# Attention's exponentials left unscaled until the output, its longest key block reduced over two banks, and the MLP run in four width groups

## The chip, the cores and the metric

The kernel runs on one core of a Trainium2 chip. A core has TensorE (PE in the profile, with its weight loads in a row of their own, PEld), VectorE (DVE), ScalarE (ACT), GpSimd (POOL) and SyncE (SP), which here issues the DMAs. Each engine takes its own instructions in the order in which they stand. SBUF is the working memory; PSUM, into which TensorE writes, has eight banks of 512 fp32 columns. The metric is the device time of one execution in microseconds (us).

## The reference

Three stages follow each other, all in fp32: block-causal attention, an MLP with a leaky ReLU, and a mixture of eight experts whose gates are normalised in eight rounds.

```
attention: B=4, H=8, S=576, D=64
scores = (q @ k.T) / sqrt(D), masked so that query block i sees key blocks 0..i (blocks of 64)
attn = exp(scores - max)
attn = attn / (sum(attn) + 1e-09)
x = attn @ v                         # 2304 tokens x 512
MLP: x = max(0.01 * h, h) @ w_out    # h = x @ w_in, 512 -> 2048 -> 512
experts: P = gates(x @ w_gate); out = sum over e of P[:, e] * (relu(x @ w1[e]) @ w2[e])
```

The MLP's weights come as words of another format (pairs of 32-bit words) and are turned into fp32 on the chip, eight elementwise steps for each unit of 128 columns.

## The kernel before, in words

**Attention** goes over 16 pairs of heads (four batches, four pairs each). In a pair, query block i has its scores for 64(i+1) keys made in one matmul (`score`, L313; two heads stand beside each other in the 128 output rows). Block 8, with 576 keys, doesn't fit one bank and is made as two matmuls of 288 columns in two tiles, with two maxima, two exponentials, one minimum (L317) and one sum (L324). VectorE takes the maximum of a score tile (L314), ScalarE the exponential with its running sum (L319). `normalise` then turns the sums of three blocks at a time into reciprocals (L329 on GpSimd, L330 on VectorE) and multiplies the exponentials by them in place: blocks 8 to 5 on VectorE (L337), block 4 on ScalarE (L335), blocks 3 to 0 on GpSimd (L337). The scaled exponentials are transposed on TensorE in seven groups of up to four 128x128 squares (`turn_attn`, L344), copied out of PSUM (five groups on ScalarE, L351, two on VectorE, L353) and multiplied with v (`weigh`, L366 and L369), which gives the pair's 128 features by 576 queries in a tile `av` of two banks. `split_x` writes this as a rounded high part (ScalarE, L382) and the rest (VectorE, L383). All matmuls up to here are in fp32; in the MLP and behind it each operand is a high and a low part in fp32r, and three products take the place of one.

PSUM in this stage: three banks for scores (`ps_sc`), three for transposes (`ps_tr`), two for `av`. The scores of pair p+1, the transposes and products of pair p and the q and k of pair p+2 are written side by side in one loop (`turns` lists what stands beside each score); the scheduler that builds the program then sets the order of instructions on each engine. The steps that turn the MLP's weights into fp32 (`bits_steps`) are dealt out over this loop, ten units in all.

**MLP** in two groups of 1024 hidden columns (eight units f of 128). In a group the five token blocks (three of 512 tokens, two of 384) follow each other; for each f `hidden` makes 12 matmuls (L510) and four elementwise instructions, `second` 12 matmuls (L539) into four banks that gather the eight f. At the end of a block the four banks are drained into `xa`: copied in group 0 (L548, L550), added in group 1 (L552). The weights of group 1 are turned to fp32 beside group 0, stored to DRAM (`s_in`, `s_out`), loaded again and split. The pools of this stage are opened after those of attention are closed. The last block runs beside the steps that open the experts (`x_step`, `gate_chunk`, `w1_sums`).

**Experts** (L735 and L789) take the rest of the time, and the change touches only which pool their weights come from.

Of the kernel before, what the change touches and what calls it, by code (L numbers as in the profile page):

```python
# [15 lines left out]
P = 128  # L16
BLK = 64
# [19 lines left out]
def block_attention_mlp_moe(  # L37
# [24 lines left out]
    FC = 8  # L62
    NG = DFF // (FC * P)
# [16 lines left out]
    w1pool = ctx.enter_context(tc.tile_pool(name="w1pool", bufs=4))  # L80
    wpools = {1: [w1pool, w1pool]}
    dram = ctx.enter_context(tc.tile_pool(name="dram", bufs=1, space=bass.MemoryType.DRAM))
# [18 lines left out]

    s_in = dram.tile([DM, (NG - 1) * FC * P], F32, name="s_in")
    s_out = dram.tile([(NG - 1) * FC * P, DM], F32, name="s_out")
    w_raw, w_part = {}, {}

    def w_load(which, e, j, pool=None):
        raw = (pool or rawpool).tile([P, 1024], F32, name="wraw", tag="wraw")
        f0 = 2 * j * P
        if which == 1:
            src = s_in[:, (e - 1) * FC * P + f0:(e - 1) * FC * P + f0 + 2 * P] if e < NG else w1[e - NG][:, f0:f0 + 2 * P]  # L110
            nc.sync.dma_start(
                out=raw.rearrange("p (c f) -> p c f", c=KC), in_=src.rearrange("(c p) f -> p c f", p=P)
            )
        else:
            src = s_out[(e - 1) * FC * P + f0:(e - 1) * FC * P + f0 + 2 * P, :] if e < NG else w2[e - NG][f0:f0 + 2 * P, :]
            nc.sync.dma_start(
                out=raw.rearrange("p (j d) -> p j d", j=2), in_=src.rearrange("(j p) d -> p j d", p=P)
            )
        w_raw[which, e, j] = raw

    def w_tiles(which, e, j):
        pool = wpools[which][min(j, 1)]
# [23 lines left out]
    def bits_steps(which, f):  # L146
# [35 lines left out]
        def rest():  # L182
            bf = st["bf"] = (st["b"] if f < FC else st["low"]).bitcast(F32)
# [22 lines left out]
        def store():  # L206
            a = st["af"]
            nc.gpsimd.tensor_tensor(out=a, in0=a, in1=st["bf"], op=ALU.add)
            g = slice((f - FC) * P, (f - FC + 1) * P)
            if which == 1:  # L210
                nc.sync.dma_start(out=s_in[:, g].rearrange("(c p) f -> p c f", p=P), in_=chunks(a))
            else:
                nc.sync.dma_start(out=s_out[g, :], in_=a)

        return [begin, bound, shift, sign, power, rest] + ([parts, low_part] if f < FC else [store])


    def attention(att, ps_sc, ps_tr, ps_av):
# [10 lines left out]
        nmax = [att.tile([P, NQ + 1], F32, name=f"nmax{i}") for i in range(2)]  # L229
        ssum = [att.tile([P, NQ + 1], F32, name=f"ssum{i}") for i in range(2)]  # L230
        rsum = [att.tile([P, NQ + 1], F32, name=f"rsum{i}") for i in range(2)]
# [68 lines left out]
        turn_order = [8, 0, 7, 1, 6, 2, 5, 3, 4]  # L300
        col = {i: n + 1 for n, i in enumerate(turn_order)}

        latest = [None]

        def score(p, i):
            n = BLK * (i + 1)
            cuts = [(0, n)] if n <= 512 else [(0, n // 2), (n // 2, n)]
            part = []
            nm, sm = nmax[p % 2], ssum[p % 2]
            x = col[i]  # L310
            for s, (lo, hi) in enumerate(cuts):
                sc = ps_sc.tile([P, 512], F32, name="sc", tag="sc")[:, 0:hi - lo]
                nc.tensor.matmul(sc, qbd[p % 2][:, i, :], kT[p % 2][:, lo:hi], start=True, stop=True)  # L313
                latest[0] = nc.vector.tensor_reduce(out=nm[:, x - s:x - s + 1], in_=sc, axis=AX.X, op=ALU.max, negate=True)  # L314
                part.append(sc)
            if len(cuts) > 1:
                nc.vector.tensor_tensor(out=nm[:, x:x + 1], in0=nm[:, x:x + 1], in1=nm[:, x - 1:x], op=ALU.min)  # L317
            for s, (lo, hi) in enumerate(cuts):
                nc.scalar.activation(  # L319
                    out=ex[p % 2][:, off[i] + lo:off[i] + hi], in_=part[s], func=AF.Exp,  # L320
                    bias=nm[:, x:x + 1], scale=1.0, accum_out=sm[:, x - s:x - s + 1],
                )
            if len(cuts) > 1:
                nc.gpsimd.tensor_tensor(out=sm[:, x:x + 1], in0=sm[:, x:x + 1], in1=sm[:, x - 1:x], op=ALU.add)  # L324

        def normalise(p, lo, hi):
            r, s, e = rsum[p % 2], ssum[p % 2], ex[p % 2]
            c = slice(lo + 1, hi + 1)
            nc.gpsimd.tensor_scalar(out=r[:, c], in0=s[:, c], scalar1=EPS, scalar2=None, op0=ALU.add)  # L329
            nc.vector.reciprocal(out=r[:, c], in_=r[:, c])  # L330
            for i in turn_order[lo:hi]:
                a = e[:, off[i]:off[i] + BLK * (i + 1)]
                x = r[:, col[i]:col[i] + 1]
                if i == 4:
                    nc.scalar.activation(out=a, in_=a, func=AF.Copy, scale=x)  # L335
                else:
                    (nc.gpsimd if i < 4 else nc.vector).tensor_scalar(out=a, in0=a, scalar1=x, scalar2=None, op0=ALU.mult)  # L337

        def turn_attn(p, g):
# [10 lines left out]
            if n == 4 and g not in (5,):  # L350
# [22 lines left out]

        def split_x(p):
            b, hp = divmod(p, NPAIR)
            x = av.pop(p)[:, o:o + S]
# [619 lines left out]
```

## Time and profile before

| | |
|---|---|
| time, median of 3 runs (lowest, highest) | 2136.92 us (2135.82, 2139.2) |
| time of the profiled execution | 2137.32 us |
| its span, first to last instruction | 2135.5 us |
| TensorE matmul rows busy | 2114.1 us, 99% of the span |
| TensorE weight loads busy | 1842.6 us, 86% |
| VectorE, ScalarE, GpSimd busy | 1434.7, 915.0, 500.9 us |
| mean granted TensorE clock | 0.999 |

Busy time is the time that an engine's instructions cover. Matmuls overlap one another and their ends are modelled, so that a full row of TensorE says only that it never stood without a matmul; what one costs is read from the distance between the starts of neighbours. Attention ends 234 us into the span, the MLP between 605 and 650 us, where it overlaps the start of the experts.

### The profile page before, as it was taken

The numbers are of one execution on the slowest core, as the hardware profiler recorded it, in microseconds if no ns is written. First come the engines' busy times: TensorE is split into PE (matmuls) and PEld (weight loads), VectorE is DVE, ScalarE is ACT, GpSimd is POOL, SyncE is SP. The second block draws the span as 40 slices with busy tenths as digits, with TensorE's granted clock in tenths as the row PEclk, the third lists the DMA queues.
The fourth block names the chain that finished last, engine by engine and source line by source line (L and its number), as shares of the span: only waits on it lengthen the run. The fifth ranks groups of instructions, "written<-read, shape, count | busy, mean of one in ns | idle before, by whom it ended". The sixth has DMA issues, their size and how long they took to land.

```text
span 2135.5 us, 29009 instructions
## 1 busy us (share of the span) xinstructions
PE 2114.1 (99%) x10772; PEld 1842.6 (86%) x10772; DVE 1434.7 (67%) x2347; ACT 915.0 (43%) x1900; POOL 500.9 (23%) x587
## 2 busy tenths in 40 slices
PE   8999999999999999999999999999999999999999
PEld 5665688988899889989998998899899989988998
DVE  7887656644367876667678666766678676667665
ACT  7886422232234344344444434443444344344432
POOL 3444311200031222122123212222222222122120
PEclk9999999999999999999999999999999999999999
DMA  4442122420011221222123122212222221222120
GB/s 113 97 99 74 56 70 75 120 63 1 1 47 53 79 78 41 79 79 64 56 89 99 50 69 79 77 43 79 80 61 88 79 79 48 71 79 73 47 79 30
DMA packets 157245, 146.59 MB, mean 69 GB/s; under 512 B 62640, under 2 KB 126128, under 8 KB 157104
## 3 DMA queue, kind: packets, MB, share of 16 engines
q1 hardware_dynamic: 157104, 144.75, 22.8%
q8 instruction: 84, 1.38, 0.3%
q14 instruction: 57, 0.47, 0.1%
HBM read 135.81 MB, written 8.91 MB: 68 GB/s over the span
## 4 chain that ended last, share of the span: by engine, by line
PE 95%; DVE 3%; ACT 1%; issue 0%; DMA 0%; POOL 0%; SPq 0%; ACTq 0%; POOLq 0%; DVEq 0%
PE o L789 36%; PE h_ps L735 33%; PE o L539 9%; PE h_ps L510 9%; PE sc L313 3%; PE av L369 2%; PE tr L344 2%; DVE ex L337 0%; DVE w1l L693 0%; DVE nmax L314 0%; PE km L286 0%; ACT ex L319 0%; PE qm L280 0%; PE av L366 0%; DMA wraw<-in_moe_w_out_dram 0%
## 5 line engine op out<-in xcount | busy, mean ns | idle before, releaser
L789 PE MATMUL o<-w2h,xhlate 128*128 128x512 f32 x1152 | 402.6, 390 | 0.0
L789 PE MATMUL o<-w2h,xllate 128*128 128x512 f32 x1152 | 401.6, 389 | 0.0
L676 POOL TENSOR_TENSOR wa<-wraw 128x256 f32<-128x256 f32 x96 | 88.7, 924 | 1252.4 <-DVE w1l L693 1214.7
L743 ACT COPY s<-h_ps 128x384 f32<-128x384 f32 x288 | 138.1, 480 | 538.7 <-PE h_ps L735 538.5
L752 DVE TENSOR_TENSOR c<-h_ps,s 128x384 f32<-128x384 f32 x288 | 155.6, 554 | 311.0 <-PE h_ps L735 301.0
L735 PE MATMUL h_ps<-xhS,w1h 128*128 128x384 f32 x768 | 257.1, 335 | 0.0
L735 PE MATMUL h_ps<-xlS,w1h 128*128 128x384 f32 x768 | 256.5, 334 | 0.0
L735 PE MATMUL h_ps<-xhS,w1l 128*128 128x384 f32 x768 | 256.5, 334 | 0.0
L789 PEld LDWEIGHTS o<-w2h,xllate 128*128 128x128 f32 x1152 | 216.3, 188 | 45.4
L789 PEld LDWEIGHTS o<-w2h,xhlate 128*128 128x128 f32 x1152 | 216.3, 188 | 43.4
L789 PE MATMUL o<-w2l,xhlate 128*128 128x512 f32 x576 | 224.7, 390 | 0.0
L789 PE MATMUL o<-w2l,xllate 128*128 128x512 f32 x576 | 224.4, 390 | 0.0
L802 DVE SCALAR_TENSOR_TENSOR xa<-o,pr,xa 128x512 f32<-128x512 f32 x264 | 189.1, 740 | 50.4 <-PE o L789 50.4
L735 PE MATMUL h_ps<-xhA,w1l 128*128 128x384 f32 x576 | 193.0, 335 | 0.0
L735 PE MATMUL h_ps<-xhA,w1h 128*128 128x384 f32 x576 | 193.0, 335 | 0.0
L735 PE MATMUL h_ps<-xlA,w1h 128*128 128x384 f32 x576 | 192.7, 335 | 0.0
L693 DVE TENSOR_TENSOR w1l<-wraw,w1h 128x512 fp32r<-128x512 f32 x192 | 172.9, 938 | 0.1
L693 DVE TENSOR_TENSOR w1l<-wa,w1h 128x512 fp32r<-128x512 f32 x192 | 161.9, 845 | 0.0
L758 ACT ACTIVATE xllate<-c 128x384 fp32r<-128x384 f32 x144 | 75.7, 526 | 183.4 <-DVE c L752 183.4
L132 DVE TENSOR_TENSOR w2l<-wraw,w2h 128x1024 fp32r<-128x1024 f32 x100 | 145.6, 1456 | 6.7 <-ACT w2h L131 6.7
L735 PEld LDWEIGHTS h_ps<-xhS,w1h 128*128 128x128 f32 x768 | 144.2, 188 | 0.1
L735 PEld LDWEIGHTS h_ps<-xlS,w1h 128*128 128x128 f32 x768 | 144.2, 188 | 0.0
(158 smaller groups left out, 4064.9 us busy)
## 6 DMA issues: line engine op xcount, KB each, us to landing
wraw<-in_moe_w_dram SPq DMA_DIRECT2D x192, 512.0 KB, 4.3
wraw<-in_moe_w_in_dram SPq DMA_DIRECT2D x16, 512.0 KB, 3.8
wraw<-in_moe_w_out_dram SPq DMA_DIRECT2D x16, 512.0 KB, 3.8
out_dram<-xa SPq DMA_DIRECT2D x18, 256.0 KB, 2.0
qraw<-in_q_dram SPq DMA_DIRECT2D x32, 128.0 KB, 2.8
kraw<-in_k_dram SPq DMA_DIRECT2D x32, 128.0 KB, 2.4
vraw<-in_v_dram SPq DMA_DIRECT2D x32, 128.0 KB, 2.4
s_in<-wa SPq DMA_DIRECT2D x8, 256.0 KB, 2.4
```

The lines of the kernel that those rows point to most:

```text
L132: nc.vector.tensor_tensor(out=lo, in0=raw, in1=f32(hi), op=ALU.subtract)
L313: nc.tensor.matmul(sc, qbd[p % 2][:, i, :], kT[p % 2][:, lo:hi], start=True, stop=True)
L510: nc.tensor.matmul(ps[:, 0:n], w[:, c, cols], x, start=c == 0 and s == 0, stop=c == KC - 1 and s == 2,)
L539: nc.tensor.matmul(o_ps[s][:, 0:n], w[:, cut], h[:, 0:n], start=f == 0 and m == 0, stop=f == FC - 1 and m == 2)
L676: nc.gpsimd.tensor_tensor(out=one[:, 0], in0=a21, in1=a22, op=ALU.add)
L693: nc.vector.tensor_tensor(out=lo, in0=x, in1=f32(hi), op=ALU.subtract)
L735: mm = nc.tensor.matmul(ps, w[:, c], x[:, c], start=first and c == 0 and s == 0, stop=c == 1 and s == 2, skip_group_check=True,)
L743: nc.scalar.copy(out=t, in_=bank[n, name][:, 0:HT])
L752: nc.vector.tensor_tensor(out=c, in0=x, in1=part[n, add], op=ALU.add)
L758: nc.scalar.activation(out=hi, in_=x, func=AF.Relu),
L789: mm = nc.tensor.matmul(o, h, w, start=m == 0, stop=m == 11)
L802: nc.vector.scalar_tensor_tensor(out=a, in0=o, scalar=pr[:, tt, e:e + 1], in1=a, op0=ALU.mult, op1=ALU.add)
```

## The change

In attention the exponentials are transposed and multiplied with v as they are. The reciprocals of a pair's nine totals are made at once (`totals`). GpSimd multiplies them into a 128x576 tile `by_query`, whose row r holds the reciprocals of the queries q with q = r modulo 64 and zeros elsewhere (`place_totals`). Two fp32 matmuls with a 128x128 matrix of ones for each head (`both_heads`) then give the reciprocals of all 576 queries on each head's 64 feature rows: 512 columns into a bank of `ps_tr`, 64 into a free corner of the `av` tile (`spread_totals`). They are copied to SBUF (`by_feature`), and `split_x` first multiplies `av` by them into `xs`, from which the high part (ScalarE) and the rest (now on GpSimd) are made.

The score tiles become pairs of banks, two pairs in all: block 8 fills one pair and has one maximum and one exponential over both banks; blocks 7 and 0, 6 and 1, 5 and 2, 4 and 3 share a pair. `ps_tr` has two banks in place of three. ScalarE copies transposed groups 0 and 3, VectorE the other five.

The MLP goes in four groups of 512 hidden columns; groups 2 and 3 leave out the last token block, which then runs once over all eight units of both. The weights of groups 1 to 3 are turned into fp32 parts straight into their tiles, five steps at a time beside the runs before them, without the way over DRAM. In attention eight units are turned in place of ten. `bits_steps` loses its last alternative (`store`). The later pools are opened with `reuse_waits="tile"`, by which a tile waits for those that it overlaps, not for the whole pool before it.

```diff
         def score(p, i):
             n = BLK * (i + 1)
-            cuts = [(0, n)] if n <= 512 else [(0, n // 2), (n // 2, n)]
...
-                sc = ps_sc.tile([P, 512], F32, name="sc", tag="sc")[:, 0:hi - lo]
...
+            place = next(some.index(i) for some in shares if i in some)
+            if place == 0:
+                bank[p] = ps_sc.tile([P, 2, 512], F32, name="sc", tag="sc")
...
+            latest[0] = nc.vector.tensor_reduce(out=nm, in_=sc, axis=axes, op=ALU.max, negate=True)
+            nc.scalar.activation(out=to, in_=sc, func=AF.Exp, bias=nm, scale=1.0, accum_out=sm)
...
-        def normalise(p, lo, hi):
-            r, s, e = rsum[p % 2], ssum[p % 2], ex[p % 2]
...
-                if i == 4:
-                    nc.scalar.activation(out=a, in_=a, func=AF.Copy, scale=x)
-                else:
-                    (nc.gpsimd if i < 4 else nc.vector).tensor_scalar(out=a, in0=a, scalar1=x, scalar2=None, op0=ALU.mult)
+        def totals(p):
+            r, s = rsum[p % 2], ssum[p % 2]
+            nc.gpsimd.tensor_scalar(out=r, in0=s, scalar1=EPS, scalar2=None, op0=ALU.add)
+            nc.vector.reciprocal(out=r, in_=r)
+
+        def place_totals(p):
+            nc.gpsimd.tensor_tensor(
+                out=by_query.rearrange("p (i q) -> p i q", q=BLK),
+                in0=one_head.unsqueeze(1).to_broadcast([P, NQ, BLK]),
+                in1=rsum[p % 2].unsqueeze(2).to_broadcast([P, NQ, BLK]), op=ALU.mult,
+            )
...
-            if n == 4 and g not in (5,):
+            if g in (0, 3):
                 nc.scalar.copy(out=dst, in_=tr[:, 0:n])
             else:
                 nc.vector.tensor_copy(out=dst, in_=tr[:, 0:n])
...
+        def spread_totals(p):
+            t, rb = av[p], ps_tr.tile([P, 512], F32, name="rb", tag="tr")
+            nc.tensor.matmul(rb, both_heads, by_query[:, 0:512], start=True, stop=True)
+            nc.tensor.matmul(t[:, 0:S - 512], both_heads, by_query[:, 512:S], start=True, stop=True)
+            nc.scalar.copy(out=by_feature[:, 0:512], in_=rb)
+            nc.vector.tensor_copy(out=by_feature[:, 512:S], in_=t[:, 0:S - 512])
...
-            x = av.pop(p)[:, o:o + S]
+            t = av.pop(p)
+            nc.vector.tensor_tensor(out=xs, in0=t[:, o:o + S], in1=by_feature, op=ALU.mult)
...
-                y = x[:, u0 - t0:u1 - t0]
+                y = xs[:, u0 - t0:u1 - t0]
                 nc.scalar.copy(out=hi, in_=y)
-                nc.vector.tensor_tensor(out=lo, in0=y, in1=f32(hi), op=ALU.subtract)
+                nc.gpsimd.tensor_tensor(out=lo, in0=y, in1=f32(hi), op=ALU.subtract)
...
-        tc.tile_pool(name="ps_sc", bufs=3, space=bass.MemoryType.PSUM) as ps_sc,
-        tc.tile_pool(name="ps_tr", bufs=3, space=bass.MemoryType.PSUM) as ps_tr,
+        tc.tile_pool(name="ps_sc", bufs=2, space=bass.MemoryType.PSUM) as ps_sc,
+        tc.tile_pool(name="ps_tr", bufs=2, space=bass.MemoryType.PSUM) as ps_tr,
...
+    runs = [(b, range(g, g + FG)) for g in (0, FG) for b in range(NB)]
+    runs += [(b, range(g, g + FG)) for g in (2 * FG, 3 * FG) for b in range(NB - 1)]
+    runs += [(NB - 1, range(2 * FG, NF))]
```

How the change moves instructions is seen in the order in which the scheduler puts them. First TensorE in a late pair of attention, before (tr: transposes; sc: scores of the next pair; km and qk_tail: the keys and queries of the one after it; av: products with v):

```order
L366 MATMUL av<-at,vraw_116 64x128 x2
L286 MATMUL km<-ident,kraw 128x128 x4
L292 MATMUL qk_tail<-ident,qraw 128x64
L292 MATMUL qk_tail<-ident,kraw 128x64
L369 MATMUL av<-at,vraw_116 64x448 x2
L313 MATMUL sc<-kT_119,qbd_117 128x384
L344 MATMUL tr<-ident,ex_122 128x128 x4
L369 MATMUL av<-at,vraw_116 64x448 x2
```

The same place after the change, in the line numbers of the changed kernel:

```order
L364 MATMUL av<-at,vraw_112 64x128 x2
L321 MATMUL sc<-kT_115,qbd_113 128x384
L321 MATMUL sc<-kT_115,qbd_113 128x320
L342 MATMUL tr<-ident,ex_118 128x128 x4
L287 MATMUL km<-ident,kraw 128x128 x4
L367 MATMUL av<-at,vraw_112 64x448 x2
L375 MATMUL av<-by_query,both_heads 128x64
L321 MATMUL sc<-kT_115,qbd_113 128x192
L293 MATMUL qk_tail<-ident,qraw 128x64
L293 MATMUL qk_tail<-ident,kraw 128x64
L374 MATMUL rb<-by_query,both_heads 128x512
L321 MATMUL sc<-kT_115,qbd_113 128x256
```

Two rows have come in among the others (L375 and L374, with `both_heads` as weights), once in each of the 16 pairs, and none has gone.

Then TensorE at the end of attention, before (vraw_116 belongs to the last pair; h_ps is the MLP's first product):

```order
L344 MATMUL tr<-ident,ex_122 128x128 x15
L366 MATMUL av<-at,vraw_116 64x128 x2
L344 MATMUL tr<-ident,ex_122 128x128 x4
L369 MATMUL av<-at,vraw_116 64x448 x2
L344 MATMUL tr<-ident,ex_122 128x128 x5
L369 MATMUL av<-at,vraw_116 64x448 x2
L369 MATMUL av<-at,vraw_116 64x320 x2
L369 MATMUL av<-at,vraw_116 64x192 x2
L369 MATMUL av<-at,vraw_116 64x64 x2
L510 MATMUL h_ps<-xhfirst,w1h 128x512
```

And after the change, in part:

```order
L342 MATMUL tr<-ident,ex_118 128x128 x5
L472 MATMUL h_ps<-xhfirst,w1h 128x512
L472 MATMUL h_ps<-xlfirst,w1h 128x512
...
L472 MATMUL h_ps<-xhfirst,w1h 128x512
L342 MATMUL tr<-ident,ex_118 128x128 x8
L364 MATMUL av<-at,vraw_112 64x128 x2
L472 MATMUL h_ps<-xlfirst,w1h 128x512
...
L367 MATMUL av<-at,vraw_112 64x448 x2
L374 MATMUL rb<-by_query,both_heads 128x512
L375 MATMUL av<-by_query,both_heads 128x64
L342 MATMUL tr<-ident,ex_118 128x128 x4
```

The MLP's first products, which stood behind the last pair, now stand in four stretches of 19 to 22 matmuls between its transposes and products.

## Rows read from the trace of the kernel before

**Rows 1.** The page: busy time, share and instructions; then the granted clock in 40 slices.
```profile
PE 2114.1 (99%) x10772; PEld 1842.6 (86%) x10772; DVE 1434.7 (67%) x2347; ACT 915.0 (43%) x1900; POOL 500.9 (23%) x587
PEclk9999999999999999999999999999999999999999
```

**Rows 2.** Busy time of each engine in stretches of attention and MLP.
```profile
core 0: us, PE busy (x) PEld busy (x) DVE busy (x) ACT busy (x) POOL busy (x), PEclk, DMA share, GB/s
25.78:130.55 104.77, 104.59 (x630) 64.75 (x629) 85.67 (x215) 84.48 (x250) 46.91 (x72) 1.00 0.39 94
130.55:234.28 103.73, 94.79 (x562) 57.99 (x561) 78.59 (x194) 72.30 (x216) 44.95 (x65) 0.98 0.30 75
199.03:202.44 3.41, 3.41 (x14) 2.76 (x13) 1.25 (x3) 1.66 (x6) 0.20 (x2) 0.50 0.00 0
240.00:420.00 180.00, 180.00 (x869) 158.43 (x868) 117.85 (x203) 50.93 (x90) 34.99 (x25) 1.00 0.28 84
420.00:600.00 180.00, 180.00 (x854) 153.89 (x854) 70.46 (x117) 55.72 (x98) 5.68 (x5) 1.00 0.08 25
```

**Rows 3.** TensorE's instructions in order of time: start, us, what; 100 us into attention.
```profile
100.62 0.33 PE L313 MATMUL sc<-kT,qbd 128*128 128x64 f32 x2
100.79 0.28 PE L344 MATMUL tr<-ident,ex 128*128 128x128 f32 x1
100.91 1.02 PE L313 MATMUL sc<-kT,qbd 128*128 128x512 f32 x2
101.77 1.15 PE L344 MATMUL tr<-ident,ex 128*128 128x128 f32 x9
102.75 1.14 PE L313 MATMUL sc<-kT,qbd 128*128 128x128 f32 x4
```

**Rows 4.** The same view at the start, and where pairs 1 and 9 begin their products.
```profile
5.35 1.09 PE L280 MATMUL qm<-ident,qraw 128*128 128x128 f32 x4 [5.35 <-DVE ident L454]
...
25.78 0.44 PE L366 MATMUL av<-at,vraw 128*64 128x128 f32 x4
...
87.53 0.43 PE L313 MATMUL sc<-kT,qbd 128*128 128x64 f32 x2
87.81 0.28 PE L344 MATMUL tr<-ident,ex 128*128 128x128 f32 x1
...
130.55 0.44 PE L366 MATMUL av<-at,vraw 128*64 128x128 f32 x4
```

**Rows 5.** TensorE's waits from 130 to 235 us: total, times, longest.
```profile
PE tr L344 <- ACT ex L335: 3.5, 3, 2.1
PE sc L313 <- ACT ex L319: 3.3, 3, 2.0
PE av L366 <- DVE xllate L383: 1.0, 1, 1.0
PE tr L344 <- DVE kT L275: 0.7, 1, 0.7
```

**Rows 6.** Groups of instructions in attention: count | busy us, mean ns | idle before.
```profile
L337 DVE TENSOR_SCALAR ex<-ex,rsum 128x512 f32<-128x512 f32 x15 | 11.4, 762 | 0.0
L353 DVE COPY at<-tr 128x512 f32<-128x512 f32 x16 | 10.9, 683 | 5.6 <-PE tr L344 5.6
L383 DVE TENSOR_TENSOR xlfirst<-av,xhfirst 128x576 fp32r<-128x576 f32 x8 | 6.0, 751 | 3.0 <-ACT xhfirst L382 3.0
L330 DVE RECIPROCAL rsum<-rsum 128x3 f32<-128x3 f32 x44 | 7.5, 170 | 7.5 <-POOL rsum L329 6.4
L317 DVE TENSOR_TENSOR nmax<-nmax 128x1 f32<-128x1 f32 x14 | 2.0, 146 | 0.1
L351 ACT COPY at<-tr 128x512 f32<-128x512 f32 x77 | 43.5, 601 | 10.8 <-PE tr L344 10.6
L335 ACT ACTIVATE ex<-ex,rsum 128x320 f32<-128x320 f32 x15 | 8.4, 559 | 0.7 <-DVE rsum L330 0.6
L203 POOL TENSOR_TENSOR wa<-wa,w1h 128x512 f32<-128x512 f32 x8 | 10.8, 1352 | 4.4 <-ACT w1h L199 4.0 <-DVE ex L337 0.4
```

**Rows 7.** All of VectorE's scalings in attention; the drains of the MLP's banks.
```profile
L337 DVE TENSOR_SCALAR ex<-ex,rsum 128x576 f32<-128x576 f32 (+1 forms) x64 | 37.5, 607 | 1.8
...
L552 DVE TENSOR_TENSOR xa<-o,xa 128x512 f32<-128x512 f32 (+2 forms) x20 | 10.4, 548 | 9.3 <-PE o L539 9.3
```

**Rows 8.** The chain that ended last, where attention ends: start, us, what.
```profile
232.31 1.97 PE av L369 x16
234.28 9.52 PE h_ps L510 x41
```

More of the change, by code (lines that the diff above doesn't have):

```diff
@@ L204, in low_part, with bits_list @@
             nc.gpsimd.tensor_tensor(out=st["lo"], in0=a, in1=chunks(st["bf"]), op=ALU.add)
[L206 to L211, printed above, removed]
-            else:
-                nc.sync.dma_start(out=s_out[g, :], in_=a)
-        return [begin, bound, shift, sign, power, rest] + ([parts, low_part] if f < FC else [store])
+        return [begin, bound, shift, sign, power, rest, parts, low_part]
+    def bits_list(units):
+        todo = []
+        for n, u in enumerate(units):
+            todo.append(lambda u=u: bits_load(*u))
+            if n:
+                todo += bits_steps(*units[n - 1])
+        return todo + bits_steps(*units[-1])
     def attention(att, ps_sc, ps_tr, ps_av):
@@ L454, in block_attention_mlp_moe, with hidden @@
         nc.vector.tensor_tensor(out=ident[r, r], in0=ramp[r, :], in1=turned[r, :], op=ALU.is_equal)
-    w2a = ctx.enter_context(tc.tile_pool(name="w2a", bufs=1))
+    hid = {}
+    def hidden(b, f, ps_pool, tag, h_pool, g_pool):
+        t0, n = blocks[b]
+        wh, wl = (w.rearrange("p (c f) -> p c f", c=KC) for w in w_part[1, 0, f // 2])
+        cols = slice((f % 2) * P, (f % 2 + 1) * P)
+        ps = ps_pool.tile([P, 512], F32, name="h_ps", tag=tag)
+        for c in range(KC):
+            x_hi, x_lo = x_parts(c, t0, t0 + n)
+            for s, (w, x) in enumerate(((wh, x_hi), (wh, x_lo), (wl, x_hi))):
+                nc.tensor.matmul(
+                    ps[:, 0:n], w[:, c, cols], x,
+                    start=c == 0 and s == 0, stop=c == KC - 1 and s == 2,
+                )
+        hi = h_pool.tile([P, 512], F32R, name="hh", tag="hh")
+        lo = h_pool.tile([P, 512], F32R, name="hl", tag="hl")
+        g = g_pool.tile([P, 512], F32, name="g", tag="g")
+        nc.scalar.activation(out=g[:, 0:n], in_=ps[:, 0:n], func=AF.Copy, scale=NEG_SLOPE)
+        nc.vector.tensor_tensor(out=g[:, 0:n], in0=ps[:, 0:n], in1=g[:, 0:n], op=ALU.max)
+        nc.scalar.copy(out=hi[:, 0:n], in_=g[:, 0:n])
+        last = nc.vector.tensor_tensor(out=lo[:, 0:n], in0=g[:, 0:n], in1=f32(hi[:, 0:n]), op=ALU.subtract)
+        hid[b, f] = (hi, lo)
+        return last
@@ L456, in block_attention_mlp_moe, with second @@
+    def second(b, f, s, ps, start, stop):
+        n = blocks[b][1]
+        wh, wl = (w.rearrange("p (j d) -> p j d", j=2)[:, f % 2, :] for w in w_part[2, 0, f // 2])
+        hi, lo = hid[b, f]
+        cut = slice(s * P, (s + 1) * P)
+        for m, (w, h) in enumerate(((wh, hi), (wl, hi), (wh, lo))):
+            nc.tensor.matmul(
+                ps[:, 0:n], w[:, cut], h[:, 0:n], start=start and m == 0, stop=stop and m == 2
+            )
     with (
         tc.tile_pool(name="att", bufs=1) as att,
-        tc.tile_pool(name="ps_sc", bufs=3, space=bass.MemoryType.PSUM) as ps_sc,
@@ L872, in block_attention_mlp_moe @@
             raw2 = [tc.alloc_tile_pool(name="raw2r", bufs=1, side="right", reuse_waits="tile")]
-        if e == NG - 1 and last and f in (2, 4, 6):
-            gate_chunk(NPASS - 1, f // 2 - 1, h_bank())
-    assert not bits and not later
+    assert not work and not later
     gpool.release()
```

262 lines of the change are left out of this document (111 added, 151 removed).

## The prediction

> **What bounds the kernel now.** I read the page first: TensorE's row covers 99% of the span at a granted clock of 0.9 or more in every slice [rows 1]. That alone says little, so I went to stretches. In the MLP TensorE shows no idle time in 360 us while VectorE is busy 188.31 of them and ScalarE 106.65 [rows 2]: there TensorE sets the time, and the MLP's matmuls are the same in number before and after. In attention there are two halves. From 25.78 to 130.55 us TensorE stands idle for 0.18 us, from 130.55 to 234.28 for 8.94 us [rows 2]. Then I asked whether the first half's full row is real, and read starts in place of lengths: a 512-column score, two instructions, starts at 100.91 and its successor at 101.77, nine transposes start 0.98 us before the next score [rows 3]. Everything stands close behind everything else; nothing in that half waits long for another engine. So TensorE bounds attention too, and eight pairs pass in 130.55 - 25.78 = 104.77 us [rows 4], 13.10 us each.
>
> This gives a measure of what attention loses. Sixteen pairs at 13.10 us are 209.6 us. From TensorE's first instruction at 5.35 [rows 4] to the MLP's first at 234.28 [rows 8] pass 228.9 us. 19.3 us are lost somewhere. Recorded are 8.94 us of idle time in the second half, and 1.7 us because the granted clock stood at 0.5 (1.2 of 2.4 GHz) for 3.41 us behind two idle gaps [rows 2]; the remaining 8.7 us I put down, as an estimate, to the start (first scores, first exponentials, first scalings: about 6) and to short waits in the second half (about 2.7). Of the second half's waits the largest are for ScalarE's scaling of block 4 (3.5 us), for exponentials that hold a score bank (3.3), for `split_x` (1.0) and for a copy (0.7) [rows 5].
>
> **The change part by part.**
>
> *Two fp32 products more in each pair.* The 512 columns of `rb` are priced by a score of the same shape: 0.86 us from start to start [rows 3]. The 64 columns beside it cost 0.17 us where such a score stands between transposes [rows 3] and 0.28 us where it follows a product of the other width [rows 4]; both neighbours occur, and I take 0.24. Together 1.10 us, 16 times: +17.6 us. Nothing is taken from TensorE in return: the scalings stood on other engines, and block 8 is still two matmuls. Bounds: 1.03 and 1.24 us with 0.1 us for one more change of width (the difference of the two prices), +16.5 to +19.8.
>
> *What the other engines give up.* Nearly all of it hides behind TensorE, so it counts only through waits that go. VectorE loses 37.5 us of scalings in all [rows 7], 2.3 us a pair, and a `split_x` subtraction of 0.75; it gains three copies of 0.68 and a product with `by_feature` of about 0.75 [rows 6] (same shape, same kind of operands as the subtraction), plus a small copy. That is level; two reciprocals of 0.17 and a minimum of 0.15 go as well [rows 6], so that it comes out about 0.6 us a pair lighter. ScalarE loses three copies of 0.60 and the scaling of 0.56, and gains one copy of 0.60 [rows 6]. GpSimd loses its scalings and gains `by_query` and the subtraction, 576 columns each: by the 1352 ns of a two-input job of 512 [rows 6] about 1.5 us each. ScalarE comes out about 1.8 us lighter, and GpSimd a little. With all three busy at most 82% of the first half [rows 2], the gain on the path is the waits: ScalarE's scaling no longer exists (3.5 us), `av` is freed by one VectorE product in place of ScalarE and then VectorE (1.0), the exponentials come sooner (3.3), and the clock's 1.7 us go with the gaps.
>
> *The end of attention.* The MLP's first products stand between the last pair's steps now. They cost TensorE what they did, and cover its waits there. This is again a part of the 19.3 us, not a new gain.
>
> *The start.* Transposes of the first pair wait for exponentials alone. But those must still be made one after another on ScalarE; of about 6 us I leave 4.5.
>
> *New waits.* Two banks for transposes in place of three, with `rb` as one more user; two groups of transposes stand directly behind each other and the second needs the copy of the one two before. A copy takes 0.60 to 0.68 us [rows 6], the transposes between about 0.44 (four at 0.11, from nine in 0.98 us [rows 3]) plus two short scores. Bounds: 0, and a copy's 0.6 us in each pair, 9.6 us. And `rb` waits for GpSimd's `by_query`, whose inputs are ready several us earlier: 0 to 1.5 us a pair if GpSimd is held up. I take 3 us for all, near the lower end, because ScalarE, which is late most often [rows 5], is the engine that loses most work.
>
> *MLP in four groups.* 19 runs end in a drain of four banks where 10 did: 36 drains more. One takes 0.55 us on VectorE [rows 7]; VectorE has 35% of the stretch free [rows 2], and the ten ends of before show no idle TensorE. Lower bound 0. Upper bound: nine more ends at which TensorE waits for a whole drain and a weight step before it, about 1.2 us each, 11 us. I take 1.2 us. If VectorE were full, each end would cost four drains, 2.2 us.
>
> *Weights.* Sixteen units no longer go through DRAM, and group 1's second split is gone; eight units in place of ten are turned in attention. This was work of VectorE, GpSimd and SP under a TensorE without idle time, so it counts zero. SP's loads now wait in the order of steps for a raw tile; behind such a wait stand the loads of q, k and v, which are due a pair (13 us) later, so a wait of a few us there hides. If that cover failed, the next scores would be late by the excess.
>
> *Sum.* 5.35 + 209.6 + 17.6 + 4.5 + 3 = 240.0 for the end of attention's work against 234.3: +5.8. With +1.2 in the MLP: +7. The profiled execution took 2137.32 us, 1.8 over its span, and the median of the three runs shown is 0.4 below it; 2136.92 + 7 = 2144 us.
>
> **A rule that speaks against the change.** TensorE's lost time sits beside VectorE and GpSimd, both busy in the first half for 85.67 and 46.91 of 104.77 us [rows 2], and a GpSimd job of two inputs there takes 1352 ns [rows 6]; no row tells whether VectorE was held meanwhile. The Trainium skill's page "SBUF — State Buffer" (Summary: rules for kernel authors) says that a VectorE operation with two SBUF inputs and a GpSimd operation that reads SBUF block each other for their whole length. By it the subtraction that goes to GpSimd would partly come back as blocked VectorE time. As a mechanism of this kernel it is the third rival below.
>
> **The rivals.**
> 1. *Every old wait goes and none comes.* The start keeps 4.5 us, the MLP is level: 4.2 us less than my sum, so +2.8, 2140 us. For it: the lighter engines. Against: the order is set without the chip, and the second half of before shows how it slips.
> 2. *Attention was not bound by TensorE after all*, but by a chain through VectorE, and the products hide. Then a pair shortens by what VectorE gives up, 0.6 us: -10 us, 2127 us, faster. For it: weight loads fill only 64.75 of 104.77 us against 158.43 of 180 in the MLP [rows 2]. The Trainium skill ("Trainium Kernel Development and Optimization", Performance Expectations) says that this share, not the matmul row, tells how full TensorE is. Against: the starts in [rows 3], where fp32 products leave no room between them; a long fp32 product simply needs few loads. It decides if the pitch of pairs stays at 13.1 us or below.
> 3. *GpSimd or the two transpose banks hold TensorE in each pair.* At 0.8 us a pair +13 in place of my 3: 2154 us.
>
> **How the numbers follow.** A measurement here tells about 0.2% (4.3 us) from no change, so the lines are 2132.6 and 2141.2. My forecast and its neighbourhood, 2141.2 to 2150: 0.38. Rival 3, 2150 to 2162: 0.22. Rival 1 and the low edge of my own terms, within 0.2%: 0.27. Rival 2 and whatever gain I don't see: 0.13. Slower 0.60, same 0.27, faster 0.13. The range goes from 2135, which leaves out most of rival 2, to 2158, which leaves out the far end of rival 3; the likeliest case alone spans 2140 to 2150.
>
> **What would show it.** Right: the pitch of pairs at 14.0 to 14.5 us in the first eight pairs, TensorE without idle time through all of attention, no clock of 0.5 near 200 us, `rb` at 0.86 us from start to start, the MLP's stretch without idle TensorE. Wrong: a pitch of 13.1 or below (rival 2); idle time before `tr` released by copies, or before `rb` released by GpSimd (rival 3); idle TensorE at the run ends of the MLP. The step that I trust least is that new waits stay at 3 us.

## The result and the profile after

The changed kernel takes 2160.97 us (median, 2160.86 to 2161.1) against 2136.37 beside it: +24.6 us, ratio 1.0113 (95% interval 1.0095 to 1.013). The forecast was +7, with a range that ends at 2158.

The page of the changed kernel, busy time and share of each engine, and the granted clock in 40 slices, which answer to [rows 1]:

```profile
PE 2137.5 (99%) x10836; PEld 1850.5 (86%) x10836; DVE 1436.9 (67%) x2315; ACT 895.7 (41%) x1828; POOL 503.0 (23%) x531
PEclk9999999999999999999999999999999999999999
```

TensorE has 64 instructions more, the products, and 23 us more of busy time. The shares of the span read as before and tell nothing. Stretches do. The windows view of the changed kernel (columns as in [rows 2]), cut where pair 1, pair 9 and pair 16 begin their products, where attention's last matmul starts, and at the last matmul of the MLP's groups:

```profile
27.19:147.98 120.79, 117.51 (x664) 69.89 (x663) 81.86 (x180) 74.03 (x213) 31.64 (x32) 1.00 0.31 75
147.98:255.46 107.48, 104.44 (x585) 62.58 (x584) 70.01 (x152) 62.70 (x182) 33.15 (x34) 1.00 0.27 65
255.46:275.54 20.08, 20.08 (x96) 13.74 (x95) 9.37 (x18) 5.43 (x9) 0.00 (x0) 1.00 0.00 0
275.54:664.90 389.36, 388.62 (x1910) 341.44 (x1907) 232.64 (x406) 124.78 (x226) 91.02 (x68) 1.00 0.13 40
664.90:2159.10 1494.20, 1489.90 (x7526) 1352.34 (x7524) 1029.81 (x1533) 615.54 (x1164) 341.44 (x373) 1.00 0.22 69
```

The same view of the kernel before, from the end of attention on:

```profile
234.28:641.30 407.02, 406.28 (x1984) 355.84 (x1985) 221.72 (x365) 127.18 (x225) 60.64 (x47) 1.00 0.18 55
641.30:2135.50 1494.20, 1489.92 (x7526) 1352.45 (x7524) 1032.79 (x1533) 615.65 (x1164) 339.60 (x373) 1.00 0.22 69
```

Behind the groups both kernels take 1494.20 us. The groups took 407.02 us; they take 389.36 now, and 80 of their matmuls stand inside attention (next fence). Such a matmul starts 0.227 us behind the one before it, so these are 18.2 us, and 389.36 + 18.2 = 407.5: the MLP is level. **All of the loss lies in attention.** Its own work ends 23.3 us later: its last matmul starts at 275.54 - 18.2 = 257.4 against 234.1 before (the MLP's first starts at 234.28 [rows 8]). A pair takes 120.79 / 8 = 15.10 us in the first half, 13.10 before, and 107.48 / 7 = 15.35 in the second.

The MLP's first products alone, in the stretch that attention ends in, in the same view of the changed kernel:

```profile
240.00:275.54 35.54, 19.31 (x80) 14.71 (x80) 3.45 (x5) 2.99 (x5) 1.00 0.01 1
```

TensorE's waits in the changed kernel from 25 to 255 us (line <- what it waited for: total, times, longest), and one row of the same view for the weight loads:

```profile
PE sc L321 <- ACT ex L323: 4.2, 10, 1.0
PE av L367 <- DVE at L351: 1.5, 3, 1.1
PE tr L342 <- ACT qbd L273: 0.4, 1, 0.4
...
PEld sc L321 <- ACT ex L323: 10.1, 19, 1.3
```

Against [rows 5] the waits for scalings and for `split_x` are gone; those of scores for an exponential, that is for a score bank to come free, rose from 3.3 to 4.2 us (the first half of before has no such row). Together the rows on TensorE are shorter than before, 6.1 us against 8.5, so they explain nothing of 23.3 us: a matmul's row covers short waits. The products themselves, in order of time, and the groups view of the longer one, whose idle time stands last:

```profile
92.52 0.43 PE L375 MATMUL av<-by_query,both_heads 128*128 128x64 f32 x2
92.88 0.27 PE L293 MATMUL qk_tail<-ident,qraw 64*128 64x64 f32 x1
...
94.01 1.02 PE L374 MATMUL rb<-by_query,both_heads 128*128 128x512 f32 x2
94.96 0.97 PE L367 MATMUL av<-at,vraw 128*64 128x448 f32 x4
...
L374 PE MATMUL rb<-by_query,both_heads 128*128 128x512 f32 x30 | 15.7, 605 | 0.0
```

From start to start the long one takes 0.95 us and the short one 0.36, changes of width included; over all 16 pairs the two make 19.9 us, 1.24 a pair. No idle time stands before `rb`, and no wait of TensorE or of its weight loads names `by_query`: GpSimd is not late with it.

The same distances, from each start of a TensorE matmul to the next, can be summed over attention, from the first matmul to its last. Before they make 228.9 us. In the changed kernel all but the two products and the MLP's 80 matmuls makes 231.8 us. So the loss is the products and 2.9 us more, and nothing came off the rest.

### The profile page after: what moved, and what is told of

It reads as the page before. It is cut to its first block, busy times and chain, and to the rows that moved or that the text cites. A ratio compares the mean times of both kernels' runs of the same rounds, so it can differ in the third digit from the quotient of the medians.

```text
span 2159.1 us, 28853 instructions
## 1 busy us (share of the span) xinstructions
PE 2137.5 (99%) x10836; PEld 1850.5 (86%) x10836; DVE 1436.9 (67%) x2315; ACT 895.7 (41%) x1828; POOL 503.0 (23%) x531
## 4 chain that ended last, share of the span: by engine, by line
PE 95%; DVE 3%; ACT 1%; issue 0%; POOL 0%; ACTq 0%; DVEq 0%; POOLq 0%
PE o L802 36%; PE h_ps L748 32%; PE h_ps L472 9%; PE o L492 9%; PE sc L321 3%; PE av L367 2%; PE tr L342 2%; PE rb L374 1%; ACT ex L323 1%; DVE nmax L322 0%; ACT qbd L273 0%; DVE at L351 0%; DVE w1l L706 0%; PE qm L281 0%; PE km L287 0%
## 5 line engine op out<-in xcount | busy, mean ns | idle before, releaser
L802 PEld LDWEIGHTS o<-w2h,xhlate 128*128 128x128 f32 x1152 | 216.2, 188 | 43.4
L748 PEld LDWEIGHTS h_ps<-xhS,w1l 128*128 128x128 f32 x768 | 144.2, 188 | 0.0
```

Source lines behind the costliest of these rows:

```text
L748: mm = nc.tensor.matmul(ps, w[:, c], x[:, c], start=first and c == 0 and s == 0, stop=c == 1 and s == 2, skip_group_check=True,)
L802: mm = nc.tensor.matmul(o, h, w, start=m == 0, stop=m == 11)
```

## The experiments

"Over before" is the median less that of the kernel before that ran beside it (2135.8 to 2138.0); sums below are made from this column. "Rest" is the sum of TensorE's distances just described, in the trace of each run, without the two products and the MLP's matmuls; it was 228.9 us before. Kernels marked * leave out attention's normalisation, so their time is that of the other work.

| Run | Score + transpose banks | us | Over before | Ratio [95%] | Rest |
|---|---|---|---|---|---|
| after | 2 pairs + 2 | 2160.97 | +24.6 | 1.0113 [1.0095, 1.013] | 231.8 |
| e1 old attention | 3 + 3 | 2141.84 | +3.9 | 1.0023 [1.0012, 1.0035] | 231.9 |
| e2 no products * | 2 pairs + 2 | 2152.71 | +14.7 | 1.0075 [1.006, 1.009] | 243.1 |
| e3 products, single banks | 3 + 3 | 2155.96 | +18.0 | 1.009 [1.0073, 1.0106] | 229.9 |
| e4 product twice | 2 pairs + 2 | 2175.35 | +37.4 | 1.018 [1.0165, 1.0195] | 232.8 |
| e5 no products * | 3 + 3 | 2139.52 | +3.3 | 1.0013 [1.0003, 1.0023] | 231.1 |
| e6 products | 4 + 2 | 2164.26 | +28.1 | 1.0127 [1.0111, 1.0142] | 231.6 |
| e7 copies as before | 2 pairs + 2 | 2162.08 | +25.9 | 1.0117 [1.0102, 1.0132] | 234.5 |
| e8 fp32r products | 2 pairs + 2 | 2156.11 | +19.9 | 1.0088 [1.0073, 1.0103] | 229.9 |
| e9 fp32r products | 3 + 3 | 2161.9 | +26.1 | 1.0116 [1.01, 1.0131] | 242.8 |
| e10 before, unscaled * | 3 + 3 | 2135.47 | -0.3 | 0.9997 [0.9989, 1.0006] | 229.2 |
| e11 no products * | 4 + 2 | 2126.67 | -9.1 | 0.9953 [0.9939, 0.9966] | 216.2 |
| e12 totals by DMA | 3 + 3 | 2203.71 | +67.9 | 1.0321 [1.0303, 1.0338] | 288.3 |
| e13 products in a corner | 4 + 2 | 2144.53 | +7.9 | 1.0035 [1.0022, 1.0048] | 214.9 |
| e14 the same, fp32r | 4 + 2 | 2143.67 | +7.1 | 1.0031 [1.0019, 1.0042] | 219.3 |
| e15 before, other banks | 4 + 2 | 2133.34 | -3.3 | 0.9984 [0.9975, 0.9993] | 223.4 |
| e16 old attention | 4 + 2 | 2128.35 | -8.3 | 0.9959 [0.9947, 0.9972] | 217.5 |

The granted clock differs a little among executions. Those of the kernel before with a mean of 1.0 took 2134.1 to 2136.4 us, those with 0.998 or 0.999 took 2135.7 to 2140.8; the changed kernel had 1.0 in all of its own. So differences of 2 or 3 us can be the clock alone.

**Parts of the change apart: e1 to e4.** e1 is the changed kernel with attention's code and banks of before; e2 leaves out the two products; e3 keeps them and goes back to single banks, with block 8 in two tiles, two maxima and two exponentials; e4 makes the long one twice.

```diff
 e2:
-            t, rb = av[p], ps_tr.tile([P, 512], F32, name="rb", tag="tr")
-            nc.tensor.matmul(rb, both_heads, by_query[:, 0:512], start=True, stop=True)
...
-            nc.scalar.copy(out=by_feature[:, 0:512], in_=rb)
...
+            nc.scalar.copy(out=by_feature[:, 0:512], in_=by_query[:, 0:512])
 e3:
-                bank[p] = ps_sc.tile([P, 2, 512], F32, name="sc", tag="sc")
...
+                sc = ps_sc.tile([P, 512], F32, name="sc", tag="sc")[:, 0:hi - lo]
...
-        tc.tile_pool(name="ps_sc", bufs=2, space=bass.MemoryType.PSUM) as ps_sc,
-        tc.tile_pool(name="ps_tr", bufs=2, space=bass.MemoryType.PSUM) as ps_tr,
+        tc.tile_pool(name="ps_sc", bufs=3, space=bass.MemoryType.PSUM) as ps_sc,
+        tc.tile_pool(name="ps_tr", bufs=3, space=bass.MemoryType.PSUM) as ps_tr,
 e4:
             nc.tensor.matmul(rb, both_heads, by_query[:, 0:512], start=True, stop=True)
+            nc.tensor.matmul(rb, both_heads, by_query[:, 0:512], start=True, stop=True)
```

> The changed kernel with the attention of before (scalings in place, scores in three single banks, three transpose banks), but with the changed weight steps, pools and MLP in four groups. If all of the loss sits in attention: 2130 to 2138 us, near or just under before. If the four-group MLP or its weight steps cost part of it: 2145 us or more.

> The changed kernel without the two products with both_heads; by_feature is copied from by_query instead, so that the normalisation is left out. Theory A (the products fill TensorE, which sets the pace): 1.2 to 1.3 us a pair go, 2139 to 2142 us. Theory B (the pace is set by waits for fewer and paired banks): the waits remain, 2150 us or more.

> The changed kernel with the score and transpose banks of before (three single score banks, block 8 in two halves with two maxima and two exponentials, three transpose banks); the products stay. Theory A: within 3 us of 2161. Theory B: the new waits go, 2144 to 2153 us.

> The changed kernel with the 512-column product made twice into the same bank. Theory A: 16 times 0.86 us more, 2173 to 2176 us. Theory B: TensorE has gaps of over 1 us in each pair into which part of it slips, 2162 to 2168 us.

e4 costs 37.4 - 24.6 = 12.8 us more (14.4 between the two medians), 0.8 to 0.9 us for each of 16 products: more work on TensorE is paid in full. e1 puts all but about 4 us of the loss into attention's code and banks. But e2 takes back only 24.6 - 14.7 = 9.9 of it, and e3 6.6. Without its products the changed attention is still 14.7 us slower than before.

**What the lighter engines are worth: e5, e10.** e5 is e3 with e2's edit. e10 is the kernel before without its scalings.

```diff
 e10, against the kernel before:
-            for i in turn_order[lo:hi]:
...
-                if i == 4:
-                    nc.scalar.activation(out=a, in_=a, func=AF.Copy, scale=x)
-                else:
-                    (nc.gpsimd if i < 4 else nc.vector).tensor_scalar(out=a, in0=a, scalar1=x, scalar2=None, op0=ALU.mult)
```

> Both at once: no products (by_feature copied from by_query, so the normalisation is left out) and the score and transpose banks of before. Theory C, formed from the runs so far: two bounds lie close together, TensorE's work with the products (13.8 us a pair) and the turn of the paired score banks (14.5 to 14.7 us a pair without the products), so that removing either alone gains little; with both gone the pitch falls to 13.1 to 13.5 us and the time to 2137 to 2145 us. Theory D (copies on VectorE or the GpSimd jobs hold the pace): 2148 us or more.

> The kernel before with nothing changed but that the exponentials are not scaled (the 16 scalings on ScalarE, 64 on VectorE and 64 on GpSimd are left out, so that the normalisation is left out). The prediction's credit (ScalarE's scaling and the waits behind late engines go): 10 to 15 us less, 2121 to 2128 us. The rival that the runs so far suggest (TensorE's waits are made by the order of its own instructions and come back elsewhere): within 4 us of before, 2132 to 2140 us.

Nothing: e5 takes 0.6 us less than e1, whose attention has the scalings, and e10 takes 0.3 less than the kernel before. Of the two e10 is the clean one: in e5 GpSimd holds up a step of VectorE (told behind the list below). The windows view of e10, cut like [rows 2] at pairs 1 and 9 and at the end of attention:

```profile
24.50:135.20 110.70, 107.03 (x637) 65.75 (x636) 68.73 (x184) 83.12 (x243) 22.22 (x41) 1.00 0.37 89
135.20:234.40 99.20, 94.85 (x561) 56.67 (x562) 63.64 (x169) 71.55 (x215) 20.52 (x38) 1.00 0.32 78
```

VectorE loses 17 us of work in the first half (85.67 before) and GpSimd half of its own. The half-speed stretch is gone, and the first products come 1.3 us sooner. Yet the first half takes 110.70 us in place of 104.77, the second 99.20 in place of 103.73, and attention ends at the same 234.4. Its waits, in the view of [rows 5], from 25 to 255 us:

```profile
PE sc L313 <- ACT ex L319: 6.7, 9, 1.0
PE av L359 <- ACT at L344: 1.1, 1, 1.1
```

The waits for scalings are gone, but scores now wait longer for their banks: 6.7 us, where the same stretch of the kernel before has 3.3.

**Banks: e6, e11, e15, e16.** e6 is the changed kernel with four single score banks and its two transpose banks, e11 the same without products. e15 changes two numbers in the kernel before, e16 the same two in e1.

```diff
 e6 and e11, against e3 and e5; e15, against the kernel before; e16, against e1:
-        tc.tile_pool(name="ps_sc", bufs=3, space=bass.MemoryType.PSUM) as ps_sc,
-        tc.tile_pool(name="ps_tr", bufs=3, space=bass.MemoryType.PSUM) as ps_tr,
+        tc.tile_pool(name="ps_sc", bufs=4, space=bass.MemoryType.PSUM) as ps_sc,
+        tc.tile_pool(name="ps_tr", bufs=2, space=bass.MemoryType.PSUM) as ps_tr,
```

> The changed kernel with four single score banks (block 8 in two halves) in place of two pairs, and its two transpose banks. If it is the pairing, by which a bank comes free only with its partner, that holds TensorE: 2153 to 2157 us as with three single banks. If the single-bank kernel gained by its third transpose bank: 2159 to 2163 us.

> The changed kernel without the products (by_feature copied from by_query, normalisation left out), four single score banks and two transpose banks. If the two transpose banks make what the paired-bank kernel without products lost (13 us): 2149 to 2155 us. If it was the pairing of score banks: 2138 to 2143 us.

> The kernel before, with four score banks and two transpose banks in place of three and three, and no other edit; nothing left out. If the fourth score bank, with the MLP's start that then stands among the last pair's steps, makes what the unscaled kernel without products gained: 2124 to 2130 us, under both kernels. If that gain needs the unscaled exponentials: 2134 to 2140 us.

> The attention of before with four score banks and two transpose banks, in the changed MLP with its weight steps; nothing left out. As the run beside it if the MLP in four groups costs nothing: 2124 to 2131 us. 4 us above it if the changed weight steps cost what they seemed to cost with three and three banks.

e2 and e11 own the same number of banks and do the same work, but for block 8's second maximum and exponential with their minimum and sum, which only e11 has; e2 takes the score banks in pairs. That costs 14.7 + 9.1 = 23.8 us. TensorE's and its weight loads' waits in e2, then TensorE's in e11:

```profile
PE sc L321 <- ACT ex L323: 9.4, 29, 1.0
PE km L287 <- DVE at L351: 2.3, 9, 0.3
...
PEld sc L321 <- ACT ex L323: 25.2, 42, 0.7
```

```profile
PE tr L346 <- DVE at L355: 1.5, 3, 0.7
PE km L289 <- DVE at L355: 1.0, 3, 0.3
PE av L371 <- DVE at L355: 0.3, 1, 0.3
```

A pair of banks is free only when both of its exponentials have run. With single banks no row has a score on TensorE that waits for one, and the weight loads of scores wait 2.9 us for them in place of 25.2. e16 has the scalings and is as fast as e11, which has none (-8.3, -9.1): once more the scalings cost nothing on the path. The same two numbers take 14.4 us off the rest with the scalings (e1 to e16) and 14.9 without (e5 to e11, where that hold goes as well). In every kernel here with four score banks, single or in pairs, MLP products stand inside attention's end (82 matmuls in e15 and in e16); with three and three there is none. So it is the banks that give the covered end, not the changed MLP. e16 is faster than both kernels. Of e15's 3.3 us some 2 may be the clock: it had 1.0 in all executions, and those of the kernel before beside it with 1.0 took 2134.3 to 2136.4 us against its 2133.34.

With products the single banks give nothing, though: e6 takes 3.5 us more than the changed kernel. TensorE's waits in e6:

```profile
PE tr L346 <- DVE at L355: 7.1, 8, 1.7
PE sc L315 <- ACT ex L322: 5.3, 14, 0.8
```

**Where the products stand: e13, e14, e12.** The transposes wait for their banks in e6, and `rb` is a user of these. e13 is e6 with the products as twice 288 columns in the free corner of `av`, the second of them two turns of the loop later; e14 makes them of two fp32r parts. e12 drops the products: the totals go over DRAM and come back spread over the rows.

```diff
 e13, against e6:
-            t, rb = av[p], ps_tr.tile([P, 512], F32, name="rb", tag="tr")
...
+            t, cut = av[p][:, 0:S // 2], slice(n * S // 2, (n + 1) * S // 2)
+            nc.tensor.matmul(t, both_heads, by_query[:, cut], start=True, stop=True)
 e14, against e13:
-            nc.tensor.matmul(t, both_heads, by_query[:, cut], start=True, stop=True)
+            for m, b in enumerate(by_query):
+                nc.tensor.matmul(t, both_heads, b[:, cut], start=m == 0, stop=m == 1)
 e12, against e3:
+                nc.sync.dma_start(
+                    out=by_feature[p % 2][h * D:(h + 1) * D, :],
+                    in_=tot[p % 2][h].unsqueeze(0).to_broadcast([D, S]),
+                )
```

> Four single score banks, two transpose banks, and the products (fp32, 288 columns twice) in the free corner of the av tile, so that no transpose bank is taken for them; nothing left out. If the products cost TensorE's time alone and their bank did the rest of the 37 us that they cost in this layout: 2141 to 2146 us (2126.7 + 16 x 1.0). If they cost waits wherever they stand: 2152 us or more.

> The same with the products in two fp32r parts of 288 columns; nothing left out. If TensorE's time alone is left: 16 x 0.55 us over the kernel without products, 2133 to 2138 us, level with before. If the two jobs of GpSimd come late: 2145 us or more.

> The changed kernel with the banks of before, in which by_feature comes by two pairs of small DMAs through DRAM (nine totals of 128 rows written out, then read back to 64 rows each) in place of place_totals and the two products, with nothing left out. If the DMAs hide behind a pair: 2137 to 2143 us, as without products. If SP's queue holds the loads of q, k and v behind them: 2148 us or more.

e13 takes 20.2 us off e6 and needs 7.9 + 9.1 = 17.0 us more than e11, about the products' own price. TensorE's waits in e13:

```profile
PE sc L315 <- ACT ex L322: 0.6, 3, 0.3
PE tr L346 <- DVE at L355: 0.4, 1, 0.4
```

On TensorE's row the products make 20.2 us in e13 and 22.1 in e6; the rest is 16.7 us shorter in e13. So with four single score banks the products cost 17.0 us, and their place in a transpose bank, with the other split, 20.2 more. e12 is a miss by far (+67.9). VectorE's waits in it, from 25 to 300 us, and TensorE's:

```profile
DVE xs L382 <- DMA by_feature<-tot: 45.7, 13, 5.3
...
PE tr L349 <- DVE at L358: 28.1, 12, 5.6
PE sc L314 <- ACT ex L321: 13.2, 5, 3.7
```

The totals come back late, VectorE stands before `xs`, the copies of transposes stand behind it, and TensorE waits for these. Its granted clock fell as well, to a mean of 0.986 to 0.990; an estimate from that shortfall, 0.012 of 2203.71 us, puts up to 26 of the 67.9 us on it.

**Copies and parts: e7, e8, e9.** e7 lets ScalarE copy five groups of transposes, as the kernel before. e8 and e9 make the products of two fp32r parts, in the changed kernel and in e3; GpSimd then makes `by_query` twice, and VectorE has two small steps more in each pair.

```diff
 e7:
-            if g in (0, 3):
+            if n == 4 and g not in (5,):
 e8, and e9 against e3:
+            for b, r in zip(by_query, rhalf):
+                nc.gpsimd.tensor_tensor(
...
-            nc.tensor.matmul(rb, both_heads, by_query[:, 0:512], start=True, stop=True)
...
+            for n, b in enumerate(by_query):
+                nc.tensor.matmul(rb, both_heads, b[:, 0:512], start=n == 0, stop=n == 1)
```

> The changed kernel with the copies of transposed groups dealt out as before (five on ScalarE, two on VectorE). If late copies on VectorE hold TensorE: 2153 to 2158 us. Theory C (score banks wait for exponentials on ScalarE): ScalarE gets 1.8 us a pair more and the turn of the score banks longer, 2161 to 2172 us.

> The changed kernel with the products in two fp32r parts (the reciprocals split into a high part and a rest), so that 512 columns cost two passes of about 0.227 us in place of 0.86 us. Theory A (TensorE's work alone): 0.45 us a pair less, 2152 to 2155 us. Theory C: the turn of the score banks at 14.5 us a pair holds the pitch up, 2155 to 2159 us.

> The changed kernel with the score and transpose banks of before and the products in two fp32r parts. If TensorE's work and the banks are the two causes and add up: 2140 + 16 times 0.5 us = 2146 to 2150 us. If the fp32r form gains nothing where the banks are not short: 2154 us or more.

Who copies is nearly without effect. e8 gains 4.7 us; e9 loses 8.1 against e3 with the same edit, and e14 gains 0.8 against e13. So the same edit is worth -5, +8 or -1 us. TensorE's own share did fall: its row has 16.6 us of products in e8 in place of 19.9, and 13.1 in e14 in place of 20.2. In e9 most of the loss can be the clock: its four executions had a mean of 0.995 to 0.998, where e3 had 1.0 in all, and an estimate from that shortfall, 0.0025 of 2161.9 us, puts up to 5 us on it. e14 had 0.999 throughout, e13 1.0. What else e14 loses, I did not settle.

## Why the prediction was wrong

The forecast made attention +5.8 of three terms: products +17.6, new waits +3, and -14.8 for old waits that go (19.3 us lost, of which the start keeps 4.5). With the MLP's 1.2 the change without products and new waits should have given -13.6. Three runs take +24.6 apart in the same way: all but products and banks +3.3 (e5), products on three and three banks 18.0 - 3.3 = +14.7, the change of banks 24.6 - 18.0 = +6.6. In the other order (e5, e2, the changed kernel) the banks make 11.4 and the products 9.9; the +3.3 stays.

**The step that failed** is "the gain on the path is the waits". It was to bring 14.8 us, and brought none: 3.3 against -13.6 is 16.9 us of an error of 17.6. (e5 has GpSimd's hold in it; e10 has none, and its -0.3 shows no gain either.) On TensorE's row the forecast for the rest was 209.6 + 4.5 + 3 = 217.1 us, and 231.8 were measured. Two things were wrong in it. I took 13.10 us a pair as what TensorE needs and everything above as lateness of other engines; but e10, with the same matmuls and far less other work, runs its first half at 110.70 / 8 = 13.84 us, and e1, with the attention and the banks of before, at 14.12 (its pairs 1 and 9 begin their products at 25.75 and 138.68 us). No other run without the products was under 13.38 (e11). The 13.10 belonged to how one order of instructions ran, not to the work. And a wait's row names the last releaser only: with the scalings gone the same matmuls waited for banks. The lost time itself was there: beside the changed MLP two numbers of the banks bring it back, with the scalings in place (217.5 us in e16; in the kernel before they bring a part, 223.4 in e15). That 217.5 is so near the forecast is chance, for nothing in the forecast worked by banks.

The other steps:
- *TensorE bounds attention*, so extra matmuls are paid: right (e4). The second rival, 2127 us, fell with it. Its sign, the weight loads' low share, is not refuted as a sign: 63.75 of 105 us in e16 and 66.06 in e11, which wait little, 59.06 in e2, which waits more. The Trainium skill, as the prediction cited it (page "Trainium Kernel Development and Optimization", Performance Expectations), names the weight loads' busy share as a good metric of how close a kernel is to roofline; these three shares agree with it. But in the changed kernel the share is 69.89 of 120.79 us, and fp32 products still cost their full time.
- *Products +17.6*: 19.9 us on TensorE's row, at the upper bound; 14.7 as e3 less e5 and 17.0 as e13 less e11. Right in size.
- *The other engines get lighter*: right. VectorE 85.67 of 104.77 us before, 81.86 of 120.79 now; ScalarE 84.48 and 74.03; GpSimd 46.91 and 31.64. It was worth nothing on the path (e10).
- *New waits +3*: 6.6 us, within the bounds of 0 and 9.6, but probably for another reason than the one given. The transpose banks were expected; the largest recorded wait is that of scores for paired score banks. That pairing the score banks is a cost of its own stood nowhere in the prediction. It makes 23.8 us between e2 and e11, though with products and `rb` in a transpose bank it does not show (e6).
- *The start keeps 4.5*: missed by 2.9 us. The first products begin at 27.19 us, 1.4 later than before, where 1.5 sooner was forecast. In e10 they begin at 24.50.
- *The covered end*: it came, but it is due to the banks.
- *MLP +1.2, weights 0*: the MLP is level, 407.02 and 407.5 us. The weights' zero is doubtful: e1, whose attention is that of before beside the changed steps, starts its last product with v at 237.1 us in place of 234.1. *The clock's 1.7 us*: no stretch at 0.5 any more, as said.
- *Rival 1*, 2140 us: its products and its MLP came as stated, its waits did not go.
- *Rival 3*, 2154 us, was nearest, and half right: with single score banks, transposes and `rb` in two banks do hold TensorE (e6 and e13); GpSimd does not in the changed kernel. Its cited rule, VectorE held by GpSimd, comes below.
- *What would show it*: the pitch came out at 15.10 us, above the 14.0 to 14.5 that were named; the products account for 1.24 of the 2.0 over before, and e1 stands 1.0 above it without any.

**VectorE beside GpSimd.** The traces do show VectorE held. Four rows, duration in ns (shortest, median, longest): block 8's minimum of one column in e3 and in e11, then two steps of the changed kernel's MLP with the same shapes, `g`, which reads PSUM and SBUF, and `hl`, which reads SBUF alone:

```profile
L320 DVE TENSOR_TENSOR nmax<-nmax,nmax x16: 151/755/1351, 10.9 to 233.1; 128x1 f32<-128x1 f32 x16
...
L320 DVE TENSOR_TENSOR nmax<-nmax,nmax x16: 97/153/160, 11.2 to 203.5; 128x1 f32<-128x1 f32 x16
...
L480 DVE TENSOR_TENSOR g<-h_ps,g x75: 542/681/695, 285.8 to 658.8; 128x512 f32<-128x512 f32 x43, 128x384 f32<-128x384 f32 x32
L482 DVE TENSOR_TENSOR hl<-g,hh x76: 547/692/1583, 284.4 to 659.9; 128x512 fp32r<-128x512 f32 x44, 128x384 fp32r<-128x384 f32 x32
```

In e3 and e5 14 of the 16 minima end 14 to 21 ns behind a GpSimd job that began before them, mostly the subtraction that the change gave to GpSimd; in e11 none meets such a job. The Trainium skill ("SBUF — State Buffer", Summary: rules for kernel authors) says that of a VectorE operation with two SBUF inputs and a GpSimd operation that reads SBUF the second to start waits until the first is done. The traces agree. In e3 and e5 the exponentials of block 8 wait for that minimum, so these two understate what single banks and lighter engines are worth. The changed kernel has no such minimum: by an estimate from durations with and without a GpSimd job beside them, VectorE is held for some 3 us of its attention, against some 13 before, more than half of these in the scalings. That gain was worth nothing on the path either.

**What stays open.** Effects here don't add: the same score banks are worth 23.8 us without products and -3.5 with them. e1 is 3.9 us slower than the kernel before with the same attention code, and e16 5.0 faster than e15 by the same difference, which is mostly the weights' steps and the opened pools. The order of instructions around attention thus makes some 5 us either way for reasons I did not take apart. How much of e16's gain is the fourth score bank and how much the covered end was not tried apart, nor were the opened pools' `reuse_waits`. The changed kernel also takes the blocks of a pair in another order (8, 7, 0, 6, 1 and so on in place of 8, 0, 7, 1, 6), which e2 to e9 and e11 to e14 keep; no run tried it by itself.

## What to carry to other kernels

Waits that a profile lays on an engine are no credit until a kernel without that engine's work has been run: here the scalings, 17 us of VectorE in half of attention, were worth nothing, while two numbers that deal PSUM banks were worth 3.3 us in the kernel before (e15) and 12.2 in the changed MLP (e16 against e1). Ask for each bank who holds it until when; two tiles in one allocation hold both until the later one is read, and a new user in a short ring can delay the others (e6 and e13). Work added to the engine that bounds was paid in full (e4), so put its price against gains that an experiment has shown, not against the sum of idle time.

## What the runs showed of the hardware

An fp32 matmul of 128x512 costs TensorE 0.86 us from start to start ([rows 3]), and 0.8 to 0.9 when it is simply doubled (e4); one fp32r matmul of 512 columns in the MLP starts 0.227 us behind its neighbour. By that two fp32r parts in place of one fp32 product should save about half; on TensorE's row they saved 7.1 of 20.2 us in e14, and the kernel kept 0.8 of it. A VectorE minimum of one column with both inputs in SBUF took 153 ns (median, e11), and 755 in e3, where it ended 14 to 21 ns behind a GpSimd job; a step of 512 columns with one input in PSUM never took more than 695 in the changed kernel's MLP. GpSimd's `by_query`, with both inputs broadcast, took 1176 ns for 576 columns, less than the 1352 ns of a plain two-input job of 512 in [rows 6].
